# Batch 2's attention as float32 groups in a fused attention and MLP kernel

## The chip, the cores and the metric

The kernel runs on one core of a Trainium2 chip. The time is device microseconds of one execution, as a median over executions, lower is better. The engines are TensorE (PE in the profile: matmuls; PEld: its weight loads), VectorE (DVE), ScalarE (ACT), GpSimd (POOL) and SyncE (SP), which here only issues DMAs.

## The reference

Four batches, eight heads, 576 positions, head dimension 64; then two blocks on rows of 512 features. Everything is float32 in and out.

```
rel = pos[:, None] - pos[None, :]
mask_local = (rel >= 0) & (rel < 32)                     # heads 0 to 3
mask_strided = (rel >= 0) & (pos[None, :] % 32 == pos[:, None] % 32)   # heads 4 to 7
attn = softmax(where(mask, q @ k.T / 8, -1e9));  x = concat over heads of attn @ v

h = relu(x @ w_in);  u, v = halves of h;  v_n = layer norm of v
x2 = (u * (w_spatial @ v_n + b_spatial)) @ w_out

theta = x2 @ w_theta
y = x2 + w_tok_r @ (x2 * cos(theta)) + w_tok_i @ (x2 * sin(theta))
out = y + relu(y @ w_ch)
```

A position attends to at most 63 keys of its neighbourhood (local heads) or to at most 18 keys of its own class modulo 32 (strided heads, whose positions are sorted by class beforehand), so both kinds are computed in small diagonal blocks.

## The kernel before, in words

**The main work.** The matmuls of the two blocks run on float16 pairs: each float32 operand is split into a high and a low part, and three products (high·high, low·high, high·low, `PASS`) are added in PSUM. A batch's stages are, by the names of their tiles: `v` (`main_v`: 60 matmuls of 512 columns), `u`, `sp`, `x`, `th` (`main_mid`: 96, 112, 96 and 96 matmuls of 288 columns) and `y`, `c` (`main_end`: 216 and 96 of 288). The order of the stages at the end of the file is v of batch 0, then for each batch b: u, sp, x, th of b; `drain(b + 1)`; v of b + 1; y, c of b. So batch 2's attention must be done before v of batch 2, which follows th of batch 1. The stages' PSUM tiles come from one pool of three (`ps_m`). `z_chunk` takes a theta tile out of PSUM (ACT: turns; DVE: `ta<-th`, fraction), computes sine and cosine on ACT and splits z into `vn`; DMA transposes bring it to `zf`.

**Two kinds of attention.** `attention0` and `attention1(b)` work in float32, without splitting: nine groups (`groups`) of four local blocks or four to six strided blocks (one group has two local blocks). A group goes through a three-step pipeline in `attention1`: `gr_scores` (PE: two matmuls of 64 queries for each block, and the mask added by matmuls with a bfloat16 identity, into the one bank `sc`), `gr_shift` (DVE: maximum, and subtraction into `sm`), `gr_exp` (one ACT instruction), `gr_turn` (PE: transposes into the one bank `av`; ACT: copy to `pT`), `gr_pv` (PE: product with v into `av`, whose columns of ones give the sums; DVE: reciprocal and scaling), `gr_out` (PE: transposes into `sc`; ACT and DVE: high and low part into `xT`). `attention(b)` works on float16 pairs in eleven units of four blocks: `prep_qk` splits q and k (ACT: high part; DVE: low part, `qT<-qs`, `kt<-ks`), `prep_v` splits v (`vT<-vs`); `att_scores` (PE, then for each block a DVE instruction and an exponential on ACT with its sum), `att_norm` (DVE: division and low part; ACT: high part `ph`; a DMA transpose into `pT`), `att_pv` (PE, then ACT and DVE into `xT`). Batches 0 and 1 are of the first kind, batches 2 and 3 of the second: `N32` (line 33) is the number of batches in float32, and `_layout` lays the inputs out by it.

**When a step is given out.** Attention is a generator; `others` (called after each piece of main work) gives out its next step when the main work's own count of columns, divided by 2400 (`now`), has passed `ATT_AT[b][0] + n * ATT_AT[b][1]` for the n-th step (line 55). On that scale v of batch 1 lies at 59.5 to 71.0, y and c of batch 0 at 71.0 to 108.5, u to th of batch 1 at 108.5 to 156.5. A float32 attention has 13 steps, a float16 one 16. What a step gives out gets its place on each engine from the framework's scheduler, which lets `hv`, `ha`, `hg` (the main work's instructions on DVE, ACT and POOL) go 200 places ahead; so an instruction can stand earlier than the step that gave it out. All loads but three at the start go through SP's queue, in order.

The float32 attention keeps q and k in the buffers `kts` (two head pairs at a time) and v in the two buffers of tag `vT`; the float16 attention uses the same two `kts` for its split k and the same tag for its split v.

Of the kernel before, what the change touches and what calls it, by code (L numbers as in the profile page):

```python
# [29 lines left out]
TURN = 6.283185  # L30
TURNS = 1.0 / (PS * 2 * math.pi)
AHEAD = 200
N32 = 2
LAG16 = 3
V_ORDER = (0, 1, 2)
E_WAY = 'aaaadaaadaa'
# [15 lines left out]
E_YHI = 'vaavvaav'  # L52
E_ZLO = 'vvvvvvvv'
WARM = 6
ATT_AT = (None, (2.7, 3.9), (74.5, 4.4), (169.9, 4.6))
CONV_SP = (20.0, 9.9, 1.9)
CONV_OUT = (37.0, 12.0, 5.0)
CONV_TH = (49.0, 12.0, 5.0)
# [7 lines left out]
def kernel(  # L66
# [53 lines left out]
    B, DM, S = out.shape  # L120
# [28 lines left out]
    def copy(eng, key, dst, src):  # L149
        e = eng[key]  # L150
        if key == "a":
            e.activation(dst, src, AF.Copy)
        else:
            e.tensor_copy(dst, src)
# [50 lines left out]
    def pa(tag):  # L205
        return ps_a.tile([P, 512], F32, tag=tag, name=tag)

    def pa4(tag):
        return pa(tag).rearrange("p (n k) -> p n k", n=4)
# [128 lines left out]
    def prep_qk(b, hp, j, tiles):  # L338
# [7 lines left out]
        qs = att_p.tile([P, S], F32, tag="qs", name="qs")  # L346
        nc.sync.dma_start(qs, qd[b - N32, hp, :, j, :])
        ks = att_p.tile([P, S + STRIDE], F32, tag="ks", name="ks")
        nc.sync.dma_start(ks[:, 0:nk], (kl_d[b - N32, hp] if local else ks_d[b - N32, hp - 2])[:, j, :])
        copy(N, E_QHI, qT[:, j], qs)  # L350
# [78 lines left out]
    def load_qk(b, hp, q, k, c0, c1, by=None):  # L429
        by = by or nc.sync  # L430
        local = hp < 2
        src = kzl[b, hp] if local else kzs[b, hp - 2]
        k0, k1 = (c0 + STRIDE if c0 else 0, c1 + STRIDE) if local else (c0, c1)
        by.dma_start(q[:, c0:c1], qp[b, hp][:, c0:c1])
        for j in range(2):
            h = slice(64 * j, 64 * j + 64)
            by.dma_start(k[h, k0:k1], src[h, j, k0:k1])

    def load_vl(b, hp, v):
        src = vl_d[b, hp].rearrange("p n j d -> p n (j d)")  # L440
        c = slice(1, VW - 1)
        nc.gpsimd.memset(v[:, 0:9, 0:VW:VW - 1], 1.0)
        nc.sync.dma_start(v[0:96, 0:9:3, c], src[0:96, 0:6:2])
        nc.sync.dma_start(v[0:64, 1:9:3, c], src[64:128, 0:6:2])
        nc.sync.dma_start(v[64:96, 1:9:3, c], src[32:64, 1:6:2])
        nc.sync.dma_start(v[0:96, 2:9:3, c], src[32:128, 1:6:2])

    def load_vs(b, v, hps=(2, 3)):

        src = vs_d[b].rearrange("h p n j d -> p h n (j d)")  # L450
        c = slice(1, VW - 1)
        hs = slice(hps[0] - 2, hps[-1] - 1)
        for n in range(len(hps)):
            nc.gpsimd.memset(v[:, n, 0:6, 0:VW:VW - 1], 1.0)
        for i in range(11):
            k, end = CB * i, min(CB * i + CB, S)
            o = 0
            while k < end:
                n = max(range(5), key=lambda n: (SOFF[n] <= k) * (min(SOFF[n] + P, end) * 8 - n))
                m = min(end, SOFF[n] + P) - k  # L460
                p0 = k - SOFF[n]
                if i < 10:
                    r = 64 * (i % 2) + o
                    nc.sync.dma_start(v[r:r + m, :, i // 2, c], src[p0:p0 + m, hs, n])
                else:
                    for u, hp in enumerate(hps):
                        r = 64 * (hp - 2) + o
                        nc.sync.dma_start(v[r:r + m, u, i // 2, c], src[p0:p0 + m, hp - 2, n])
                k += m
                o += m  # L470
# [111 lines left out]
    def gr_out(b, g, xn, xt):  # L582
        local, blocks = groups[g]
        xh = xT[b % 2]
        for i in range(len(blocks) // 2):
            nc.tensor.transpose(xt[:, P * i:P * i + P], xn[:, i, :], ident)
        runs = []
        for i, (hp, blk) in enumerate(blocks):
            if runs and runs[-1][0] == hp and (local or blk < 10):
                runs[-1][3] += 1  # L590
            else:
                runs.append([hp, blk, i, 1])
        for hp, blk, i, n in runs:
            src = xt[:, QB * i:QB * (i + n)]
            if local:
                dst = [xh[:, e, hp, QB * blk:QB * (blk + n)] for e in range(2)]
            else:
                nr = min(3, STRIDE - 3 * blk)
                dst = [xh[:, e, hp, :].rearrange("p (j r) -> p j r", r=STRIDE)[:, :, 3 * blk:3 * blk + n * nr]
                       .rearrange("p j (n r) -> p j n r", r=nr) for e in range(2)]  # L600
                src = src.rearrange("p (n c) -> p n c", c=QB)[:, :, 0:nr * NCLS].rearrange(
                    "p n (r j) -> p j n r", j=NCLS)
            nc.scalar.activation(dst[0], src, AF.Copy)
            nc.vector.tensor_tensor(dst[1], src, dst[0], ALU.subtract)
# [56 lines left out]
    def attention1(b):  # L661
        q, k, v = {}, {}, {}

        def load_a(hp):
            q[hp], k[hp] = kts[hp % 2][:, 0], kts[hp % 2][:, 1]
            load_qk(b, hp, q[hp], k[hp], 0, S)

        def load_b(hp):
            v[hp] = att_p.tile([P, 9, VW], F32, tag="vT", name="v32", bufs=2)
            if hp < 2:  # L670
                load_vl(b, hp, v[hp])
            else:
                load_vs(b, v[hp][:, 0:6].unsqueeze(1), (hp,))

        load_a(0)
        load_b(0)
        yield
        load_a(1)
        load_b(1)
        loads = {4: (load_a, 2), 6: (load_b, 2), 7: (load_b, 3)}  # L680
        un, xs = {}, {}
        for s in range(NG + 3):
            if s < NG:
                sm = att_p.tile([P, 384], F32, tag="sm", name="sm", bufs=2)
                pT = att_p.tile([P, 4, P], F32, tag="pT", name="pT32", bufs=2)
                st = att_p.tile([P, 2, 6], F32, tag="st", name="st", bufs=4)
                un[s] = (sm, pT, st)
            if s >= 3:
                gr_out(b, s - 3, xs.pop(s - 3), pa("sc"))
            if 2 <= s < NG + 2:  # L690
                sm, pT, st = un.pop(s - 2)
                pv = pa("av")[:, 0:3 * VW].rearrange("p (i n) -> p i n", i=3)
                gr_pv(s - 2, v, pT, pv, st, pT)
                xs[s - 2] = pT
            if s < NG:
                sm, pT, st = un[s]
                sc = pa("sc")
                gr_scores(s, q, k, sc)
                gr_shift(s, sc, sm, st)
                gr_exp(s, sm)  # L700
            if s in loads:
                f, hp = loads[s]
                f(hp)
                if s == 4:
                    load_a(3)
            if 1 <= s <= NG:
                sm, pT, st = un[s - 1]
                gr_turn(s - 1, sm, pa4("av"), pT)
            yield
# [37 lines left out]
    def attention(b):  # L747
        qk, vts, pTs = {}, {}, {}
        lv = load_v(b, 0)
        prep_qk(b, 0, 0, qk)  # L750
        yield
        prep_qk(b, 0, 1, qk)
        vts[0] = prep_v(lv)
        yield
        cur = None
        qk_at = {0: (1, 0), 1: (1, 1), 3: (2, 0), 4: (2, 1), 6: (3, 0), 7: (3, 1)}
        v_at = {2: 1, 5: 2, 8: 3}
        for s in range(NU + LAG16):
            if s + 1 in v_at:
                lv = load_v(b, v_at[s + 1])  # L760
            if s >= LAG16:
                att_pv(b, s - LAG16, pTs.pop(s - LAG16), vts)
            if 1 <= s <= NU:
                pTs[s - 1] = att_norm(b, cur)
            if s < NU:
                cur = att_scores(s, qk)
            if s in qk_at:
                prep_qk(b, *qk_at[s], qk)
            if s in v_at:
                vts[v_at[s]] = prep_v(lv)  # L770
            yield
# [273 lines left out]
    timed(list(sq_parts(wth, w_th)) + [switch], *CONV_TH)  # L1045
    timed([lambda i=i: tok_part(i, (raw2, raw1)[i // 2 % 2]) for i in range(0, NZ, 2)], *CONV_TOK)
    timed(sq_parts(wch, w_ch), *CONV_CH)
    atts = [None, attention1(1)] + [attention(b) for b in range(N32, B)]
    att = {"b": 1, "n": 0}

    def now():
        return clock[0] / 2400.0
# [9 lines left out]
    def others():  # L1062
        while conv and conv[0][0] <= now():
            conv.pop(0)[1]()
        while att["b"] < B and ATT_AT[att["b"]][0] + att["n"] * ATT_AT[att["b"]][1] <= now():
            step()
# [61 lines left out]
def _layout(inputs):  # L1128
# [5 lines left out]
    def pairs(a):  # L1134
        t = a[N32:].transpose(0, 1, 3, 2).reshape(B - N32, a.shape[1] // 2, 2, D, -1)
        t = np.stack([t, t], axis=2)
        t = t.transpose(0, 1, 2, 4, 3, 5)
        return t.reshape(B - N32, a.shape[1] // 2, 2 * D, 2, -1)

    def stacked(a):  # L1140
        return a[:N32].transpose(0, 1, 3, 2).reshape(N32, a.shape[1] // 2, 2 * D, -1)

# [52 lines left out]
```

## Time and profile before

| | |
|---|---|
| median of 3 runs | 511.12 us (508.06 to 514.11) |
| the profiled execution | 509.92 us |
| its span, first to last instruction | 508.1 us |
| mean granted clock of TensorE | 0.992 of full speed |
| busy | PE 476.3 us, DVE 318.0, ACT 295.0, POOL 95.9 |

Starts are counted from the first instruction of the span; the profiled execution's time is 1.8 us longer than the span. A busy stretch of PE is the union of its matmuls' modelled times. The time that a piece of PE's work takes from the others is read from starts: from the start of its first matmul to the start of what follows. All instructions carry line 103 (a helper records them), so they are told apart by their tiles' names: `th<-x2h,wth` is a theta matmul, `sc<-kt` a float32 score, `sc<-kt,qT` a float16 score. A float32 matmul appears as two instructions.

### The profile page before, as it was taken

The page shows a single profiled execution, that of the slowest core. Times are in us where ns is not written, and L with a number is a line of the kernel's source. Part 1 is how long each engine was busy: PE and PEld are TensorE (multiplying, and loading weights), DVE is VectorE, ACT ScalarE, POOL GpSimd, SP SyncE. Part 2 cuts the span into 40 slices and gives each one's busy share as a digit, 9 for nine tenths or more (in the row PEclk, how much of TensorE's full clock was granted, in tenths as well). Part 3 has the DMA queues.
Part 4 walks back from the last instruction along what each step waited for, and adds up shares of the span by engine and source line. Part 5 has one row for each costly group of instructions (what it writes and reads, how often), then busy time and mean ns, then how long its engine had stood idle before and what let it go on. Part 6 is the DMA issues. An engine that isn't in the chain of part 4 may idle for free. (4 is left out here: it accounts for less than half of the span.)

```text
span 508.1 us, 10713 instructions
## 1 busy us (share of the span) xinstructions
PE 476.3 (94%) x4300; PEld 355.8 (70%) x4300; DVE 318.0 (63%) x714; ACT 295.0 (58%) x576; POOL 95.9 (19%) x87
## 2 busy tenths in 40 slices
PE   7889989997899789998999989999999999999996
PEld 5655757775468567776758877777657778777774
DVE  3766987557779888885399588862587121228312
ACT  2657788588995558775672767654852022158102
POOL 2042057226124410021003210021005200210220
PEclk9999999999899999998999999999999999999999
DMA  6869738456593256653170156230260020004402
GB/s 179 268 208 246 263 139 261 131 159 214 158 212 74 44 152 167 156 137 115 27 175 13 27 131 197 44 63 1 46 141 1 1 93 1 1 1 82 106 1 94
DMA packets 80296, 57.56 MB, mean 113 GB/s; under 512 B 60404, under 2 KB 66932, under 8 KB 80246
## 3 DMA queue, kind: packets, MB, share of 16 engines
q1 hardware_dynamic: 79942, 56.27, 41.4%
q8 instruction: 34, 0.56, 0.5%
q10 hardware_dynamic: 304, 0.61, 0.4%
q14 instruction: 16, 0.13, 0.1%
HBM read 37.72 MB, written 4.72 MB: 84 GB/s over the span
## 5 line engine op out<-in xcount | busy, mean ns | idle before, releaser
L103 PE MATMUL y<-wtok,zf 128*128 128x288 f16 x864 | 107.7, 286 | 1.9 <-DMA zf<-vn 1.8
L103 PEld LDWEIGHTS <-zf 128*128 128x128 f16 x864 | 83.8, 98 | 24.8 <-DMA zf<-vn 2.8
L103 PE MATMUL th<-x2h,wth 128*128 128x288 f16 x384 | 49.6, 292 | 4.7 <-DVE ta L103 4.7
L103 PE MATMUL sp<-wsp,vn 128*128 128x288 f16 x384 | 51.5, 286 | 1.6 <-ACT vn L103 1.3
L103 PE MATMUL c<-x2h,wch 128*128 128x288 f16 x384 | 48.8, 286 | 3.3 <-ACT o L103 3.3
L103 PE MATMUL x<-zf,wout 128*128 128x288 f16 x384 | 51.6, 292 | 0.0
L103 POOL TENSOR_TENSOR x2h<-x2f,x2h 128x576 f16<-128x576 f32 x20 | 26.6, 1331 | 127.8 <-issue 56.5
L103 PE MATMUL u<-xT,win 128*128 128x288 f16 x384 | 49.7, 286 | 0.0
L103 PE MATMUL v<-win,xT 128*128 128x512 f16 (+1 forms) x240 | 48.4, 380 | 0.8 <-DVE xT L103 0.6
L103 PEld LDWEIGHTS <-wth 128*128 128x128 f16 x384 | 38.1, 100 | 15.1 <-DVE ta L103 4.9
L103 PEld LDWEIGHTS <-vn 128*128 128x128 f16 x416 | 39.9, 98 | 12.1 <-ACT vn L103 1.4
L103 PEld LDWEIGHTS <-wch 128*128 128x128 f16 x384 | 37.3, 98 | 12.9 <-issue 3.8
L103 PEld LDWEIGHTS <-wout 128*128 128x128 f16 x384 | 37.3, 100 | 10.6
L103 PEld LDWEIGHTS <-win 128*128 128x128 f16 x384 | 37.3, 98 | 9.1
L103 ACT ACTIVATE sm<-sm,st 96x128 f32<-96x128 f32 (+1 forms) x88 | 34.2, 391 | 10.9 <-DVE st L103 10.8
L103 PEld LDWEIGHTS <-xT 128*128 128x128 f16 (+1 forms) x240 | 21.0, 100 | 25.2 <-issue 2.2
L103 ACT ACTIVATE x2h<-x2f 128x576 f16<-128x576 f32 (+1 forms) x28 | 20.9, 747 | 28.1 <-DVE x2f L103 27.7
L103 POOL TENSOR_TENSOR zf<-u,zf 128x576 f16<-128x576 f32 x8 | 10.7, 1339 | 107.8 <-ACT zf L103 105.1
L103 DVE SCALAR_TENSOR_TENSOR x2f<-y,x2f 128x576 f32<-128x576 f32 x16 | 12.0, 752 | 26.2 <-PE y L103 26.1
L103 ACT ACTIVATE o<-c 128x576 f32<-128x576 f32 (+1 forms) x17 | 10.3, 612 | 30.3 <-PE c L103 30.0
L103 DVE TENSOR_TENSOR ta<-ta,x2f 128x1152 f32<-128x1152 f32 x16 | 21.5, 1353 | 10.1 <-ACT ta L103 10.1
L103 DVE TENSOR_TENSOR u<-u,sp 128x576 f32<-128x576 f32 x16 | 12.0, 750 | 23.4 <-PE sp L103 23.3
(140 smaller groups left out, 780.5 us busy)
## 6 DMA issues: line engine op xcount, KB each, us to landing
qs<-in_qd_dram SPq DMA_DIRECT2D x16, 288.0 KB
out_dram<-o SPq DMA_DIRECT2D x15, 288.0 KB
ks<-in_kl_dram SPq DMA_DIRECT2D x8, 304.0 KB
ks<-in_ks_dram SPq DMA_DIRECT2D x8, 288.0 KB
x2f<-in_w_in_dram SPq DMA_DIRECT2D x2, 1024.0 KB
zf<-in_w_in_dram SPq DMA_DIRECT2D x2, 1024.0 KB
xT<-in_w_ch_dram SPq DMA_DIRECT2D x2, 1024.0 KB
vs<-in_vl_dram SPq DMA_DIRECT2D x4, 384.0 KB
```

The costliest lines, as they stand in the source:

```text
L103: ins = f(*args, **kwargs)
```

## The change

Batch 2's attention is made by `attention1(2)` in place of `attention(2)`. Its 13 steps are given out from 79.0 on, one each 5.4 (to 143.8), in place of 16 steps from 74.5 on, one each 4.4 (to 140.5). `_layout` puts batch 2's q, k into the float32 layout. Batches 0, 1 and 3 keep their kind and their times.

```
-N32 = 2
+N32 = 3
...
-ATT_AT = (None, (2.7, 3.9), (74.5, 4.4), (169.9, 4.6))
+ATT_AT = (None, (2.7, 3.9), (79.0, 5.4), (169.9, 4.6))
...
-    atts = [None, attention1(1)] + [attention(b) for b in range(N32, B)]
+    atts = [None] + [attention1(b) for b in range(1, N32)] + [attention(b) for b in range(N32, B)]
```

DVE at the theta stage of batch 0, before: `xT_95<-sc` ends batch 1's attention, `kt`, `qT` and `vT` split batch 2's first q, k and v, the `ISA` rows are its first blocks' masks and maxima.

```order
L103 TENSOR_TENSOR xT_95<-sc,xT_95 128x18x12
L103 TENSOR_TENSOR kt_80<-ks,kt_80 128x608
L103 TENSOR_TENSOR qT<-qs,qT 64x576
L103 SCALAR_TENSOR_TENSOR vT<-vs,vT 128x768
L103 ISA sm,st<-sc,mask 96x128
L103 ISA st 96x1
```

The same place now; `wx` is a weight conversion, the three `ta` take theta tiles out of PSUM, the last two rows are the first group's maxima and subtraction (`gr_shift`).

```order
L103 TENSOR_TENSOR xT_95<-sc,xT_95 128x18x12
L103 SCALAR_TENSOR_TENSOR wx<-xT_94,wx 128x576
L103 SCALAR_TENSOR_TENSOR ta_1549<-th_1493,ta_1549 128x576
L103 SCALAR_TENSOR_TENSOR ta_1566<-th_1494,ta_1566 128x576
L103 SCALAR_TENSOR_TENSOR ta_1602<-th_1577,ta_1602 128x576
L103 TENSOR_REDUCE st<-sc 128x4
L103 TENSOR_TENSOR sm<-sc,st 128x384
```

The three splits and two blocks' masks stood between `xT` and the conversion with the theta tiles behind it; now nothing stands between, and attention's DVE work comes after the theta tiles.

PE at the end of the y stage of batch 0, now: the product with v of group 0 (`av<-v`), the scores of group 2 and their masks, then the `c` matmuls.

```order
L103 MATMUL y_2005<-wtok,zf 128x288
L103 MATMUL av<-v_1854,pT_1928 64x65 x8
L103 MATMUL sc<-kt_81 64x96 x8
L103 LDWEIGHTS identb
L103 MATMUL sc<-mask_100,identb 128x96
L103 LDWEIGHTS identb
L103 MATMUL sc<-mask_100,identb 128x288
L103 LDWEIGHTS wch
L103 MATMUL c_2098<-x2h,wch 128x288
```

Before, the same place held 12 float16 products with v (`av<-pT,vT`) and the 8 float16 scores of a unit (`sc<-kt_81,qT`).

DVE in the sp stage of batch 1, now: `u` gates, `xT`, `st`, `pT`, `sm` of batch 2's groups, and the splits of batch 3's k and v (`kt<-ks`, `vT<-vs`).

```order
L103 TENSOR_TENSOR u_2346<-u_2346,sp_2590 128x576
L103 TENSOR_TENSOR kt_81<-ks,kt_81 128x608
L103 TENSOR_TENSOR u_2414<-u_2414,sp_2622 128x576
L103 TENSOR_TENSOR xT_94<-sc,xT_94 128x18x18
L103 TENSOR_SCALAR st<-av 128x6
L103 RECIPROCAL st<-st 128x6
L103 TENSOR_TENSOR pT_2417<-av,st 128x384
L103 TENSOR_REDUCE st<-sc 128x4
L103 SCALAR_TENSOR_TENSOR vT<-vs,vT 128x768
L103 TENSOR_TENSOR sm<-sc,st 128x256
```

Batch 3's splits keep their place by time, and now stand among the instructions of batch 2's groups in place of those of its float16 units.

## Rows read from the trace of the kernel before

**Rows 1.** The page: busy us (share of the span), instructions.

```profile
PE 476.3 (94%) x4300; PEld 355.8 (70%) x4300; DVE 318.0 (63%) x714; ACT 295.0 (58%) x576; POOL 95.9 (19%) x87
```

**Rows 2.** Timeline of PE, stage starts: start us, us, line, operation, tiles, count.

```profile
144.91 17.82 PE L103 MATMUL y<-wtok,zf 128*128 128x288 f16 x144
...
252.03 11.94 PE L103 MATMUL v<-win,xT 128*128 128x512 f16 x60
263.91 13.40 PE L103 MATMUL y<-wtok,zf 128*128 128x288 f16 x108
...
351.59 11.92 PE L103 MATMUL th<-x2h,wth 128*128 128x288 f16 x96
363.35 11.94 PE L103 MATMUL v<-win,xT 128*128 128x512 f16 x60
```

**Rows 3.** PE's waits, 118.3 to 252: us in total, times, longest us.

```profile
PE th L103 <- DVE ta L103: 4.7, 1, 4.7
PE sc L103 <- DVE st L103: 3.8, 2, 3.4
PE av L103 <- DVE xT L103: 2.5, 1, 2.5
PE c L103 <- ACT o L103: 1.1, 1, 1.1
```

**Rows 4.** Timeline of PE around the two stalls with a slow clock after them.

```profile
122.97 0.87 PE L103 MATMUL sc<-kt,qT 128*96 128x128 f16 x8
128.56 4.64 PE L103 MATMUL th<-x2h,wth 128*128 128x288 f16 x24 [4.72 <-DVE ta L103]
...
230.25 0.52 PE L103 MATMUL av<-pT,vT 128*64 128x126 f16 x12 [2.53 <-DVE xT L103]
230.71 6.23 PE L103 MATMUL x<-zf,wout 128*128 128x288 f16 x36
```

**Rows 5.** Stretches, PE alone: us, PE busy (instructions), granted clock, DMA share, GB/s.

```profile
127.70:131.10 3.40, 2.54 (x11) 0.59 0.80 261
...
230.00:234.00 4.00, 3.75 (x26) 0.59 0.95 260
```

**Rows 6.** Timelines of DVE and ACT in the theta stage of batch 0.

```profile
121.76 1.58 DVE L103 TENSOR_TENSOR kt<-ks,kt 128x608 f16<-128x608 f32 x1
...
126.42 1.40 DVE L103 SCALAR_TENSOR_TENSOR wx<-xT,wx 128x576 int32<-128x576 int32 x1
127.75 2.07 DVE L103 SCALAR_TENSOR_TENSOR ta<-th,ta 128x576 f32<-128x576 f32 x3
...
120.25 0.69 ACT L103 ACTIVATE kt<-ks 128x608 f16<-128x608 f32 x1
...
122.16 1.15 ACT L103 ACTIVATE wtok<-wx 128x1152 f16<-128x1152 f32 x1
...
123.81 0.71 ACT L103 ACTIVATE wx<-xT 128x576 int32<-128x576 uint8 x1
```

**Rows 7.** Timeline of PE in batch 1's attention: first full group, last product.

```profile
48.78 0.88 PE L103 MATMUL sc<-kt 64*64 64x96 f32 x16
49.59 0.34 PE L103 MATMUL sc<-mask,identb 128*128 128x384 bf16 x1
49.76 0.60 PE L103 MATMUL av<-ident,sm 128*96 128x128 f32 x4
...
118.19 4.94 PE L103 MATMUL th<-x2h,wth 128*128 128x288 f16 x39
```

**Rows 8.** The stretch of batch 1's attention, PE alone, columns as in rows 5.

```profile
48.78:118.19 69.41, 65.31 (x702) 1.00 0.62 202
```

**Rows 9.** PE's waits, 48.7 to 118.3, columns as in rows 3.

```profile
PE sp L103 <- ACT vn L103: 1.3, 1, 1.3
PE sc L103 <- DVE sm L103: 1.1, 2, 0.7
PE sc L103 <- DVE xT L103: 0.6, 2, 0.4
PE av L103 <- DVE pT L103: 0.5, 1, 0.5
PE sp L103 <- POOL vn L103: 0.3, 1, 0.3
PE av L103 <- DVE rs L103: 0.2, 1, 0.2
```

**Rows 10.** Groups by form: busy us, mean ns of one, idle before.

```profile
L103 PEld LDWEIGHTS sc<-kt 64*64 64x64 f32 x168 | 6.7, 133 | 4.2 <-issue 2.3 <-DVE sm L103 1.0 <-DVE xT L103 0.6
...
L103 DVE TENSOR_TENSOR kt<-ks,kt 128x608 f16<-128x608 f32 x8 | 10.7, 1341 | 0.1
```

## The prediction

> **What bounds the kernel now.** I read the page first: PE is busy for 476.3 of 508.1 us and no other engine for more than 318.0 [rows 1], so the end is set by how long PE's own sequence takes and by the holes in it. The change therefore has two sides: float32 groups cost PE more matmul time than float16 units, and they may take away holes.
>
> The timeline of PE shows what the stages cost. Batch 3's 96 theta matmuls take from 351.59 to 363.35, 11.76 us, or 0.1225 us each [rows 2]. That is less than the 11.92 us which the row calls busy: the last matmul's modelled end lies 0.16 us behind the next one's start, so a real hole is 0.16 us longer than the profile's idle figure. From y of one batch to the end of theta of the next are 216 + 96 + 96 + 112 + 96 + 96 = 712 such matmuls, 87.2 us. The stretch that carries batch 2's attention lasts 252.03 - 144.91 = 107.1 us, the one that carries batch 3's 363.35 - 263.91 = 99.4 us [rows 2]. So the same float16 attention adds 19.9 us to the one and 12.2 us to the other: the difference is holes. PE's waits name them: 3.8, 2.5 and 1.1 us inside batch 2's stretch, and 4.7 us just before it, in the theta stage of batch 0, where PE waits for the DVE instruction that frees a theta tile [rows 3].
>
> Two of the holes cost more than their length. After the 4.72 us hole 24 matmuls take 4.64 us where 24 x 0.1225 + 0.16 = 3.10 is usual, after the 2.53 us hole 36 take 6.23 where 4.57 is usual [rows 4]: 1.5 and 1.7 us. In both places the granted clock is 0.59 on average over the stretch [rows 5], that is, part of it at 1.2 in place of 2.4 GHz.
>
> So batch 2's attention as it is costs: 19.9 us in its stretch; in the theta stage 128.56 - 122.97 = 5.6 us from its first scores to the next theta matmul [rows 4]; and 1.5 us of slow clock. **Together 27.0 us.** About 10.7 of these are PE's own work, batch 3's 12.2 less its one 1.5 us hole.
>
> **The change, part by part.**
>
> *PE's work added.* Batch 1's attention is the same program as batch 2's will be. From the first full group's scores at 48.78 to the theta matmul after its last product at 118.19 are 69.41 us [rows 7]. In between stand 96 u, 112 sp, 96 x and 33 theta matmuls, 337 x 0.1225 = 41.3 us. PE is busy for 65.31 of it [rows 8], so 4.1 us are idle, in eight pieces [rows 9], which with 8 x 0.16 make 5.4. What is left is 22.7 us. Group 0 was scored before; its scores cost as much as the next group's, 49.76 - 48.78 = 1.0 [rows 7]. Float32 attention thus takes **23.7 us of PE without its waits**, 13.0 more than the float16 one. This includes what each break in a run of float16 matmuls costs and the hidden weight loads.
>
> One rule speaks against such a step. A float32 weight load takes 133 ns on average [rows 10], yet 16 scores with their loads take 49.59 - 48.78 = 0.81 us, 51 ns each [rows 7]: the loads lie beside other work. The Trainium skill ("TensorE: Matmul & The Clock Gate", section "Weight-path perf modes") says that the fast weight load is not used for float32. If the loads were exposed, 160 scores would cost 160 x (133 - 51) = 13 us more; the row already contains whatever they cost, so I keep 23.7.
>
> *The theta stage.* DVE's chain before: batch 2's splits begin at 121.76, and with two blocks' masks they hold DVE until the conversion at 126.42; the theta tile follows at 127.75 [rows 6]. The order of the change has none of this in front. The conversion then waits for ACT alone. There k, q and v splits go (from 120.25 to 122.16, 1.9 us), so the ACT conversion that ended at 124.5 ends at 122.6, or at 123.3 if the conversion ahead of it waits for DVE. Add DVE's 1.3 us (127.75 - 126.42) and 0.7 for the first of three theta instructions: 124.6 to 125.4. PE reaches this point at 122.97 + 1.0 (group 0's scores) = 123.95. A hole of 0.7 to 1.5 us stays; I take **1.5 with the 0.16**, from the upper end since POOL's conversions also pass there. Bounds: 0, and the whole 4.9 if something else holds the tile.
>
> *Batch 2's own stalls.* The 3.8, 2.5 and 1.1 us [rows 3] belong to the float16 chain: exponentials block by block, the splits, the `o` of stage c behind exponentials on ACT. They go. In their place come the hand-offs of the one `sc` and the one `av` bank, for each group six passes between PE and DVE or ACT. Batch 1 shows their price: waits of 1.1, 0.6, 0.5 and 0.2 us in six pieces [rows 9], 3.4 us with the 0.16. There DVE and ACT also convert weights. Batch 2 has none of that after its first group, but batch 3's splits. I take half, **1.7 us**; bounds 0.3 and 3.4, and the rival below for more.
>
> *DMA.* Eleven transposes of probabilities and 16 larger loads of q and k become some 46 smaller loads on SP's queue. Batch 1 made the same loads between weight loads, and PE waited for none of them in its stretch [rows 9]. I count nothing: between the last scores from a `kts` buffer and the first from its next contents the new order has 60 main matmuls, 7.4 us. If that cover is too short, each of the two refills costs the rest.
>
> *Batch 1's stretch.* Batch 2's first splits of q, k and v stood on DVE and ACT there. Batch 3's first two q splits take the place of batch 2's, but k and v splits go. I count -0.4 us, between 0 and -1.
>
> *The sum.* 23.7 + 1.5 + 1.7 = 26.9 us against 27.0, and -0.4: **-0.5 us**. From the profiled execution's 509.92 this gives 509.4. The median of the runs, 511.12, lies 1.2 above that execution, so I forecast **510.5 us** for a median. The holes bought 13.0 us and the float32 matmuls spend them.
>
> **Rivals.**
>
> *Faster: the holes vanish altogether.* The new order cuts the float16 runs into fewer pieces than in batch 1, theta does not wait, banks are always free: 23.7 - 0.8 + 0 + 0.3 = 23.2, -1.0 in batch 1, and -0.5 in batch 3, whose q splits come earlier. That is -5.3 us, 505.5. For it: DVE and ACT lose more than 20 us of work here. Against: batch 1 shows six waits in nine groups.
>
> *Slower: batch 3's splits sit in the bank chain.* In the sp and x stages DVE has four `kt` and two `vT` splits of batch 3 among the groups' steps, each of which holds the only `sc` or `av` bank. A `kt` split takes 1.34 us on average [rows 10], 1.58 in the theta stage [rows 6]. If six of them lie on the chain, 8 us, and one such hole brings a slow clock of 1.7: +9.7 - 1.7 - 0.5 = +7.5, 518.6. It decides from 2.2 us of hand-off waits on for slower at all, from 7.3 on for over 1%. Against: the sp order leaves PE 18 to 28 main matmuls (2.2 to 3.4 us) after most scores.
>
> *The theta stall stays.* If ACT's or POOL's conversions held the tile, not DVE's splits, 4.9 in place of 1.5 and the slow clock again: +4.9, less 0.5, 515.5. For it: POOL's conversions end late there. Against: DVE's rows put the splits right ahead of the conversion and the theta tile [rows 6].
>
> *A short hole is enough for a slow clock.* The trace has a slow spell after 2.53 us of idling but none after the 3.4 us one [rows 3, 4]. If the 1.5 us hole brings one too, +1.5: 512. The Trainium skill (the page named, section "Part 1: The HAM clock gate") says that idling brings the clock down to half; this trace agrees in two places (0.59, rows 5) and shows that length alone does not decide.
>
> **How the numbers follow.** Forecast within some 3 us of 510.5: 0.62. Holes vanish: 0.13. Splits in the chain: 0.11. Theta stall or clock: 0.14, nearly all of it within 1%. Over 1% (5.1 us, about what a measurement of this kernel can tell from no change): faster 0.12, slower 0.12, same 0.76. The range takes in the bounds (-4.5 from hand-offs, theta and batch 1; +5 from theta and hand-offs) around 510.5, widened by 1 to 2 us, as single runs before lay 3 us on either side of their median: 504 to 517.
>
> **What would show it.** Right: the wait of theta for `ta` near 128 falls to 0.7 to 1.5 us without a slow spell; y to theta of batch 1 lasts 110.5 to 113 us in place of 107.1, with waits of `sc` and `av` below 3.4 us in all; batch 3's stretch stays at 99.4. Wrong: waits of PE on `kt` loads, a slow clock in the sp or x stage, or float32 pieces longer than in batch 1.

## The result, and the profile after

The changed kernel takes 506.47 us (median of 20 runs, 504.17 to 509.03), the kernel before 511.99 on the same chip (20 runs, 508.06 to 517.15). The ratio is 0.9902, 95% interval 0.988 to 0.9924: 1.0% faster, just at the bound that I had drawn between no change and faster. The time lies inside my range, 4 us below my forecast. The profiled execution takes 506.96 us, with a span of 505.1.

The page of the changed kernel, busy time, answers to [rows 1]:

```profile
PE 485.1 (96%) x4460; PEld 364.4 (72%) x4460; DVE 284.8 (56%) x607; ACT 267.8 (53%) x475; POOL 92.9 (18%) x91
```

PE works 8.8 us longer, in a span that is 3.0 us shorter. PE's waits from theta of batch 0 to v of batch 2, against [rows 3]:

```profile
PE th L103 <- DVE ta L103: 2.0, 1, 2.0
PE sc L103 <- DVE xT L103: 0.4, 1, 0.4
```

[rows 3] begins at 118.3; with a wait of 0.4 us of `sc` for `xT` just ahead of it, the kernel before has 12.5 us. Of these 2.4 are left. The timeline of PE: group 0's scores, the theta tile that waits, and the two ends of batch 2's stretch [rows 2, 4].

```profile
122.56 0.88 PE L103 MATMUL sc<-kt 64*64 64x96 f32 x16
123.37 0.34 PE L103 MATMUL sc<-mask,identb 128*128 128x96 bf16 x2
125.73 3.56 PE L103 MATMUL th<-x2h,wth 128*128 128x288 f16 x15 [2.02 <-DVE ta L103]
...
142.10 1.15 PE L103 MATMUL y<-wtok,zf 128*128 128x288 f16 x8
...
250.10 11.94 PE L103 MATMUL v<-win,xT 128*128 128x512 f16 x60
```

The stretch lasts 108.00 us where it lasted 107.1. The theta tile's place and that stretch by windows, PE alone, columns as in rows 5:

```profile
125.50:128.90 3.40, 3.17 (x14) 0.50 0.74 259
142.10:250.10 108.00, 108.00 (x1077) 1.00 0.26 73
```

In batch 2's stretch PE is never idle. The theta hole of 2.02 us has a stretch at 0.50 (1.2 GHz) behind it. Its chain on ACT and DVE:

```profile
121.25 0.73 ACT L103 ACTIVATE xT<-xT 128x576 f32<-128x576 f32 x1 [1.65 <-DMA xT<-in_w_ti_dram]
...
122.94 0.72 ACT L103 ACTIVATE wx<-xT 128x576 int32<-128x576 uint8 x1
...
123.69 1.32 DVE L103 SCALAR_TENSOR_TENSOR wx<-xT,wx 128x576 int32<-128x576 int32 x1 [2.60 <-ACT wx L103]
124.94 1.41 DVE L103 SCALAR_TENSOR_TENSOR ta<-th,ta 128x576 f32<-128x576 f32 x2
```

Read upwards, the theta tile waits for DVE's conversion, that for ACT's, and that for the load of w_ti. Batch 2's splits, which had this place in [rows 6], are gone, and DVE idles for 2.60 us.

### The profile page after: what moved, and what is told of

The parts are those of the page before. It is cut to its first block, busy times and chain, and to the rows that moved or that the text cites. A ratio compares the mean times of both kernels' runs of the same rounds, so it can differ in the third digit from the quotient of the medians.

```text
span 505.1 us, 10834 instructions
## 1 busy us (share of the span) xinstructions
PE 485.1 (96%) x4460; PEld 364.4 (72%) x4460; DVE 284.8 (56%) x607; ACT 267.8 (53%) x475; POOL 92.9 (18%) x91
## 3 DMA queue, kind: packets, MB, share of 16 engines
HBM read 35.36 MB, written 4.72 MB: 79 GB/s over the span
## 5 line engine op out<-in xcount | busy, mean ns | idle before, releaser
L103 PE MATMUL y<-wtok,zf 128*128 128x288 f16 x864 | 107.2, 286 | 1.0 <-DMA zf<-vn 1.0
L103 PE MATMUL x<-zf,wout 128*128 128x288 f16 x384 | 49.9, 286 | 0.0
L103 POOL TENSOR_TENSOR x2h<-x2f,x2h 128x576 f16<-128x576 f32 x20 | 25.5, 1279 | 119.1 <-ACT x2h L103 47.2
L103 PEld LDWEIGHTS <-wth 128*128 128x128 f16 x384 | 38.1, 100 | 12.5 <-issue 2.2
L103 ACT ACTIVATE o<-c 128x576 f32<-128x576 f32 (+1 forms) x17 | 10.4, 616 | 32.1 <-PE c L103 31.8
L103 POOL TENSOR_TENSOR zf<-u,zf 128x576 f16<-128x576 f32 x8 | 10.7, 1340 | 86.0 <-ACT zf L103 86.0
L103 DVE TENSOR_TENSOR vn<-ta,vn 128x1152 f16<-128x1152 f32 x16 | 21.5, 1355 | 5.6 <-ACT vn L103 5.6
```

Of the source, the lines that this page charges most:

```text
L103: ins = f(*args, **kwargs)
```

## The experiments

The first theory: the kind of attention makes the gain. The first rival: the new table of due times makes it.

**E1 and E2: the two halves of the change apart.** E1 is the kernel before with the new table, E2 the changed kernel with the old table.

```
E1, against the kernel before:    E2, against the changed kernel:
-... (74.5, 4.4), ...             -... (79.0, 5.4), ...
+... (79.0, 5.4), ...             +... (74.5, 4.4), ...
```

> Batch 2's attention stays on float16 pairs, but its 16 steps are given out from 79.0 on, one each 5.4, as the change does. Theory (the gain comes from the kind: float16 splits no longer stand ahead of the theta tiles, and the float16 chain's holes in batch 2's stretch go): the splits still stand ahead of the theta conversion on VectorE, so the theta hole of 4.7 us stays, and the time is that of the kernel before, ratio 0.995 to 1.005. Rival (the pacing alone makes the gain, since the steps meet better gaps): ratio 0.988 to 0.993.

> Batch 2's attention in float32 groups, given out by the old table (74.5 on, one each 4.4). Theory (kind): most of the gain is there, ratio 0.988 to 0.994; batch 2's stretch lasts about 108 us as after the change, the theta wait is near 2 us. Rival (pacing): groups bunch, hand-offs of the two banks make PE wait over 2 us in the stretch, ratio 0.997 or more.

E1: 509.34 us, ratio 0.9959 (0.9934 to 0.9985). E2: 513.02 us, ratio 1.0031 (0.9999 to 1.0063). E1's theory holds and its rival falls: the table alone brings 0.4%, not the gain. E2's theory falls: the kind alone brings nothing. E2's rival comes true in its numbers, a ratio above 0.997 and a wait of PE of over 2 us for a bank, though one group's place makes it, as its timelines show, and not a bunching of groups. Neither half makes the gain. E1's longest waits of PE, theta of batch 0 to y of batch 1:

```profile
PE th L103 <- DVE ta L103: 5.8, 2, 4.7
PE av L103 <- DVE xT L103: 2.0, 1, 2.0
PE v L103 <- DVE ta L103: 1.7, 1, 1.7
```

With the later table the float16 units miss the 3.4 us hole of the y stage [rows 3]; the theta hole of 4.7 stays, and the end of the sixteen steps now runs into theta and v, where 1.1, 1.7 and 2.0 us are lost. E2's theta wait is 1.6 us, near the 2 expected, but PE loses 4.2 us in the y stage. Its timelines there (DVE, ACT, PE):

```profile
159.42 2.36 DVE L103 TENSOR_SCALAR vr<-vr,mv,rs 128x512 f32<-128x512 f32 x5
...
160.90 2.52 ACT L103 ACTIVATE vn<-vr 64x512 f16<-64x512 f32 x3 [4.89 <-DVE vr L103]
...
164.32 0.59 ACT L103 ACTIVATE pT<-av 96x512 f32<-96x512 f32 x1
...
164.97 0.74 PE L103 MATMUL av<-v,pT 96*64 96x65 f32 x16 [4.21 <-ACT pT L103]
```

The copy `pT<-av` frees the only `av` bank; it stands on ACT behind `vn<-vr`, which waits 4.89 us for the layer norm of v on DVE. A float32 group that begins in front of the layer norm holds its bank until the norm is done. In the changed kernel the first y-stage scores come at 162.0, and their instructions on DVE follow the norm.

**E3: batch 3 in float32 too.**

```
-N32 = 3
+N32 = 4
...
-ATT_AT = (None, (2.7, 3.9), (79.0, 5.4), (169.9, 4.6))
+ATT_AT = (None, (2.7, 3.9), (79.0, 5.4), (176.0, 5.4))
```

> Batch 3's attention in float32 groups too, its steps given out from 176.0 on, one each 5.4. Theory (what was won with batch 2 are its float16 holes, 7 us inside its stretch and 5 us at theta, while float32 costs 11 us more of matmuls): batch 3's float16 attention has only 1.5 us of holes, so its stretch grows from 99.7 to 108 to 109 us, and the time is 8 to 9 us above the changed kernel's, ratio to before 1.004 to 1.009. Rival (float32 groups are cheaper as such, because they take work off VectorE and ScalarE): ratio to before 0.985 or less.

516.66 us, ratio 1.0107 (1.0075 to 1.0139): 10.2 us above the changed kernel, where the expectation had 8 to 9 and a ratio of at most 1.009. Batch 3's stretch on PE's timeline:

```profile
260.40 1.77 PE L103 MATMUL y<-wtok,zf 128*128 128x288 f16 x13
...
369.83 1.46 PE L103 MATMUL v<-win,xT 128*128 128x512 f16 x6
```

109.4 us in place of 99.7. Where float16 has few holes to lose (1.5 us), float32 costs nearly its full price. The rival falls.

**E4 and E11: each kernel once more, unchanged.** E4 is the kernel before, E11 the changed one.

> The kernel before once more, for another profile of it. Theory (the profiled execution of before fell on the fast side: the distance of the medians is 5.5 us, that of the two profiles 3.0, because the three long holes and the slow-clock stretches behind them differ from execution to execution): the holes at theta (4.7), batch 2's x stage (2.5) and batch 3's sp stage (3.4) stand again, but their lengths or the slow stretches behind them add up to 1.5 us more or less than in the first profile. Rival (executions differ in the tail or the loads, not in these holes): holes and slow stretches the same within 0.3 us, the difference elsewhere.

> The changed kernel once more, for a second profile and a second ratio. Theory (the holes are those of the order and stand in each execution; only the slow-clock stretches behind them come and go): theta wait 1.9 to 2.2 us, no other wait over 0.7 us from th of batch 0 to v of batch 2, a stretch at 1.2 GHz behind theta or none; ratio to before 0.988 to 0.993. Rival (the first comparison was luck of the executions): ratio 0.995 or more.

E4 took 511.21 us; E11 504.87 (4 runs), ratio 0.9886 (0.9836 to 0.9936). E4's theta tile and its slow windows:

```profile
131.46 5.34 PE L103 MATMUL th<-x2h,wth 128*128 128x288 f16 x24 [4.72 <-DVE ta L103]
```

```profile
129.20:136.00 6.80, 4.54 (x20) 0.50 0.68 223
173.60:180.40 6.80, 5.80 (x29) 0.50 0.30 71
233.00:240.00 7.00, 6.21 (x67) 1.00 0.64 180
```

```profile
174.60 1.01 PE L103 MATMUL sc<-kt,qT 128*96 128x128 f16 x8 [3.42 <-DVE st L103]
```

The holes at theta (4.72) and in the y stage (3.42; the expectation puts it into batch 3's sp stage by mistake) are the same to 0.01 us in both executions. The clock behind them is not. In the first profile it falls behind theta and behind the x hole of 2.53 us [rows 5], not behind the y hole; in E4 behind theta and y, not behind an x hole of 1.62. E11's theta tile, and the windows of theta and of batch 2's stretch:

```profile
125.32 3.10 PE L103 MATMUL th<-x2h,wth 128*128 128x288 f16 x24 [1.64 <-DVE ta L103]
```

```profile
125.20:128.90 3.70, 3.58 (x27) 1.00 0.79 279
140.10:248.30 108.20, 108.14 (x1076) 1.00 0.27 76
```

The order is the same, the hole 1.64 in place of 2.02 us, less than the 1.9 to 2.2 expected, and no slow stretch follows. The 24 theta matmuls then take 2.94 us to the next start (128.26), where the first profile took 4.49. At 0.50 a slow stretch should cost half of what PE was busy in it, an estimate that fits the 1.55 us between 4.49 and 2.94: 1.6 us in the first profile of the changed kernel and 0 in E11, 3.3 and 5.2 in the two of the kernel before.

E4's theory falls all the same. From theta to y of batch 1, waits and slow clock add up to 15.8 us in the first profile and 15.5 in E4 (the table below), where it asked for a difference of 1.5. The difference lies elsewhere, as the rival has it, though the single holes and slow stretches are not the same: theta of batch 0 begins at 116.11 in place of 113.37. Ahead of it E4's clock fell twice:

```profile
20.00:26.80 6.80, 6.70 (x74) 0.50 0.63 195
67.80:71.20 3.40, 3.40 (x16) 0.50 0.00 0
```

E4's v matmuls begin at 34.64. E5, the only other profile with a slow clock between 12 and 60 us (0.51 from 22.8 to 29.7), begins them at 35.07, the other twelve between 31.66 and 32.67.

**E5 and E7: float16 with its first splits behind theta.** The splits of q, k and v of batch 2's first heads must follow the third theta tile on their engine; E7 adds a later table.

```
+            if b == 0 and m == 2:
+                last.update(a=ti, v=tf)
...
+        if b == 2 and hp == 0:
+            tc.add_manual_dep(ins.ins, last[eng].ins.name, ...)
...
E7: -... (74.5, 4.4), ...
    +... (82.0, 4.4), ...
```

> The kernel before (float16 pairs, old table), but batch 2's first splits of q, k and v must stand behind the third theta tile's instructions on ScalarE and VectorE. Theory (the gain has two parts, the theta hole, which batch 2's first splits make on VectorE, and the hole in the y stage, where attention steps meet the layer norm of v; kind and table each remove one): the theta wait falls from 4.7 us to 2 to 3, the 3.4 us wait for st in the y stage stays or grows, and about 1 to 3 us are won, ratio 0.993 to 0.999. Rival (the theta hole alone makes the gain): ratio 0.988 to 0.992. Rival (the theta hole is ScalarE's or GpSimd's conversions, not the splits): wait of 4 us or more, ratio 1.000.

> As the run before the last: float16 pairs with the first splits behind theta, and a later table too (82.0 on, one step each 4.4), so that the first scores come behind the layer norm and the last step still before theta. Theory (it is holes that were won, and float16 pairs cost 11 us less of TensorE than float32 groups): theta wait 2 to 3 us, no wait over 1.5 us in the y stage, the stretch from y to v lasts 98 to 102 us in place of the changed kernel's 108.0, ratio to before 0.974 to 0.985, faster than the change. Rival (float16 pairs bring holes wherever they stand, by their many instructions on VectorE and ScalarE): stretch 104 us or more, ratio 0.990 or more.

E5: 511.99 us, ratio 1.0028 (0.9997 to 1.0059). Its waits of PE:

```profile
PE th L103 <- DVE ta L103: 2.9, 1, 2.9
PE av L103 <- DMA pT<-ph: 2.5, 1, 2.5
PE sc L103 <- DVE qT L103: 2.3, 1, 2.3
PE sc L103 <- DVE kt L103: 1.5, 1, 1.5
```

The splits do hold the theta tile: its wait falls from 4.7 to 2.9 us. From the first theta matmul to this tile's are 15.2 us before, 12.6 in E5, and 12.9 and 12.5 in the two profiles of the changed kernel, so the splits account for all that the change won there. But they then stand in the y stage with the layer norm, and scores wait for `qT` and `kt`: the waits sum to 12.0 us, little less than the 12.5 before, and the expected 1 to 3 us are not won. E7: 512.87 us, ratio 1.0033 (1.0012 to 1.0054), with one wait of 7.9 us in the y stage; the theory falls, and the rival comes true in its numbers (ratio 0.990 or more; from y to v 112.6 us, where it has 104 or more). DVE and PE there:

```profile
167.84 2.60 DVE L103 TENSOR_TENSOR kt<-ks,kt 128x608 f16<-128x608 f32 x1
170.37 1.21 DVE L103 TENSOR_TENSOR vn<-vr,vn 128x1024 f16<-128x1024 f32 x1
...
175.80 1.01 PE L103 MATMUL sc<-kt,qT 128*96 128x128 f16 x8 [7.89 <-DVE st L103]
```

**E6 and E9: the last theta hole of the changed kernel.** The last part of w_ti gets a free piece of `zf` as its buffer; E9 adds a later table.

```
+    raw3 = zf[:, 4 * S + 5120:8 * S + 5120].bitcast(I64)
-... tok_part(i, (raw2, raw1)[i // 2 % 2]) ...
+... tok_part(i, (raw2, raw1, raw2, raw1, raw3)[i // 2]) ...
E9: -... (79.0, 5.4), ...
    +... (85.0, 5.1), ...
```

> The changed kernel with the last token weights (w_ti) loaded into a free part of zf, so that the load no longer waits for the buffer of the conversion before it. Theory (the theta wait of 2.0 us that is left, and the stretch at 1.2 GHz behind it, come from ScalarE's conversion, which waits 1.65 us for this load): the theta wait falls below 0.6 us, the slow stretch goes, 1.5 to 3.5 us less than the changed kernel, ratio to before 0.982 to 0.988. Rival (the theta tile is held by the whole chain of conversions, the load is only the first of several late steps): wait stays at 1.5 us or more, ratio that of the change, 0.988 to 0.992.

> The changed kernel with the early load of w_ti and a later table for batch 2 (85.0 on, one step each 5.1): no scores of batch 2 stand before the 162nd y matmul, so none needs VectorE while it works on the layer norm of v. Theory (two places make holes, the conversions at theta and the layer norm in the y stage; the early load clears the first, the later table the second): theta wait below 1.2 us, no wait over 1 us in the y stage, y to v of batch 2 lasts 107 to 109 us, theta to v of batch 1 13.6 us; about 3 us less than the changed kernel, ratio to before 0.981 to 0.987. Rival (a hole that is filled in one place opens in the next, whatever the table): another wait of 2 us or more between y and v, ratio 0.990 or more.

E6: 510.58 us, ratio 0.9988 (0.9966 to 1.001), so neither expectation's time came. The theta wait falls to 0.9 us, not below the 0.6 expected, and no slow stretch follows; the tile's matmuls come 10.7 us behind the first theta matmul in place of 12.9 and 12.5, so the load was the cause of most of the hole. But the order moved with it: group 0's scores left theta for the y stage, in front of the layer norm. DVE and PE there:

```profile
162.11 1.22 DVE L103 TENSOR_TENSOR vn<-vr,vn 128x1024 f16<-128x1024 f32 x1
163.24 0.55 DVE L103 TENSOR_REDUCE st<-sc 128x4 f32<-128x384 f32 x1
...
164.53 0.88 PE L103 MATMUL sc<-kt 64*64 64x96 f32 x16 [4.48 <-DVE sm L103]
```

It is E2's hole again, now at the `sc` bank. E9's later table removes it. PE's waits, theta of batch 0 to y of batch 1:

```profile
PE th L103 <- DVE ta L103: 0.9, 1, 0.9
PE sc L103 <- DVE xT L103: 0.3, 1, 0.3
```

Yet E9 takes 506.75 us, ratio 0.9916 (0.9889 to 0.9944): no faster than the change. The expected 3 us were 1.6 of a slow stretch, which E11 lacks without this edit, and 1.65 of waiting, of which E11's 1.64 leaves 0.8 to win. From theta of batch 0 to y of batch 1 E9 takes 147.1 us, E11 147.4. Behind that E9's profile loses 1.9 us, and two waits there are longer by as much: `c` waits 3.4 us for ACT's `o` (2.4 in E11), `y` 1.9 us for a DMA into `zf` (1.0). So a hole did open elsewhere, behind the stretch that the rival named.

**E8: work in the hole, nothing else.** 34 matmuls whose result nothing reads, in front of the theta tile that waits, in the kernel before.

```
+            if b == 0 and m == 3:
+                fill = pa("av")
+                for _ in range(34):
+                    nc.tensor.matmul(fill[:, 0:HS], wth[:, 0, 0, 0:P], x2h[:, 0, 0, 0:HS], start=True, stop=True)
```

> The kernel before with 34 extra matmuls of 288 columns, whose result nothing reads, in front of the theta tile that waits 4.7 us: they work for 4.2 us in the place where TensorE idled. Theory (the stretch at 1.2 GHz behind theta comes from the idling, and costs 1.6 to 2.3 us each time): theta's matmuls behind it run at 2.4 GHz, and 1.5 to 2.5 us are won although no wait was removed, ratio 0.994 to 0.998. Rival (the slow stretch has another cause, or costs nothing in the end): ratio 1.000 or more, the slow stretch still there.

PE's timeline and windows:

```profile
124.68 4.33 PE L103 MATMUL av<-x2h,wth 128*128 128x288 f16 x34
130.17 3.10 PE L103 MATMUL th<-x2h,wth 128*128 128x288 f16 x24 [1.16 <-DVE ta L103]
```

```profile
130.00:133.50 3.50, 3.33 (x26) 1.00 0.84 275
166.50:173.30 6.80, 5.13 (x27) 0.50 0.00 0
```

The theta matmuls run at 2.4 GHz, in the one place where four of four profiles with the 4.72 us hole (before, E1, E4, E12) have 0.50. So the idling makes the slow stretch here. The time, 511.20 us, ratio 1.0003 (0.9982 to 1.0024), shows no gain: the fillers pushed the first scores into the y stage, where the hole grew to 4.9 us and brought its own slow stretch. The gain in time is thus neither shown nor excluded.

**E10: float16 behind the layer norm.** E7 with E6's buffer, and a table that puts batch 2's first scores into stage c.

```
-... (74.5, 4.4), ...
+... (90.0, 4.1), ...
```

> Batch 2 on float16 pairs with its first splits behind theta, the early load of w_ti, and a table (90.0 on, one step each 4.1) that puts its first scores into the c stage, behind the layer norm. Theory (float16 pairs cost 11 us less of TensorE; the holes are those of places, and this table meets neither): no wait over 1.5 us from y to v, which lasts 98 to 102 us, ratio to before 0.970 to 0.980. Rival (float16 pairs keep VectorE too busy between y and theta, so that scores wait for st wherever they stand): waits of sc and av of 4 us or more in the stretch, 103 us or more, ratio 0.983 or more.

510.05 us, ratio 0.9975 (0.9952 to 0.9997). PE's waits:

```profile
PE c L103 <- ACT x2h L103: 5.8, 1, 5.8
PE v L103 <- DVE ta L103: 2.5, 1, 2.5
```

The scores are out of the way, the splits are not: the norm, `kt` and `qT` splits and the y tiles share DVE until 177, ACT's `x2h<-x2f` comes late, and now stage c waits. At the end attention runs into theta and v, as in E1. The theory falls. The rival has the stretch (107.2 us, where it has 103 or more) and the ratio right, but not the place: the long wait is that of `c`, not of scores.

**E12: the kernel before with two weight conversions less.**

```
-    wch = const.tile([P, 2, NC, DM], F16, name="wch")
+    wch = wth
...
-    timed(sq_parts(wch, w_ch), *CONV_CH)
```

> The kernel before without the conversion and load of the last weight, w_ch: the c matmuls read w_theta's high and low parts in its place, so two conversions (two ScalarE passes of 1.1 us, a third of 1.0 and a VectorE pass of 1.2 each, with GpSimd's low parts) are left out between theta of batch 0 and the y stage; TensorE's order is that of before, word for word. Theory (batch 2's place differs from batch 3's, whose float16 attention has one hole of 1.5 us, by the weight conversions that share VectorE and ScalarE with the layer norm and the splits in the y stage): the wait of sc for st at the y stage falls from 3.4 us to below 1.5, and y to v of batch 2 from 107.1 to 104 us or less. Rival (splits and layer norm alone overfill VectorE there): that wait stays at 2.5 us or more, y to v at 105.5 us or more.

This kernel leaves `w_ch` out: its c matmuls multiply by `w_theta`, so it computes something else than the reference. PE's waits, theta of batch 0 to v of batch 2:

```profile
PE th L103 <- DVE ta L103: 4.7, 1, 4.7
PE av L103 <- DVE xT L103: 3.6, 3, 2.5
PE c L103 <- ACT o L103: 1.5, 1, 1.5
PE sc L103 <- DVE st L103: 0.4, 1, 0.4
```

508.90 us, ratio 0.9937 (0.9912 to 0.9963). With the same order on TensorE the y-stage wait falls from 3.4 to at most 0.4 us, which the theory asked; y to v falls only to 105.0 us, where 104 or less was asked, since the x hole of 2.5 stays, with a slow clock behind it. So batch 2's place differs from batch 3's, where the same float16 attention has 1.5 us of holes, in part by the weight conversions beside it.

**All profiles side by side**, from theta of batch 0 to y of batch 1 (the third y stage), in us. Slow clock is half of PE's busy time in stretches at 0.50; the last column is the total less waits and slow clock. E8's rest holds its 34 fillers, some 4.2 us.

| | kind of batch 2 | total | waits of PE | slow clock | rest |
|---|---|---|---|---|---|
| before | float16 | 150.5 | 12.5 | 3.3 | 134.7 |
| E4 before again | float16 | 149.7 | 10.3 | 5.2 | 134.2 |
| E1 new table | float16 | 150.1 | 10.4 | 4.6 | 135.1 |
| E5 splits behind theta | float16 | 151.6 | 12.0 | 5.1 | 134.5 |
| E7 E5, table 82.0 | float16 | 151.9 | 14.6 | 3.2 | 134.1 |
| E10 E7, table 90.0 | float16 | 150.3 | 12.0 | 3.1 | 135.2 |
| E12 no w_ch | float16 | 149.7 | 10.8 | 4.4 | 134.5 |
| E8 fillers | float16 | 150.0 | 9.1 | 2.6 | 138.3 |
| after | float32 | 149.1 | 2.4 | 1.6 | 145.1 |
| E11 after again | float32 | 147.4 | 2.0 | 0 | 145.4 |
| E2 old table | float32 | 153.9 | 6.2 | 1.6 | 146.1 |
| E3 batch 3 too | float32 | 147.7 | 2.4 | 0 | 145.3 |
| E6 early w_ti | float32 | 152.7 | 5.8 | 1.7 | 145.2 |
| E9 E6, table 85.0 | float32 | 147.1 | 1.2 | 0 | 145.9 |

The account closes: whatever the order, the rest is 134 to 135 us with float16 (E8 without its fillers too) and 145 to 146 with float32. The change costs 10.8 us of PE (mean of the two profiles of each kernel), takes away 9.2 us of waits and 3.4 of slow clock: -1.9 us with the rounding. No float16 order of the table came below 10.3 us of waits, but for E8, which fills part of one; float32 has 2.4 or less wherever its first y-stage scores stand behind 162 of the 216 y matmuls, and 5.8 and 6.2 where they stand behind 126 and 108 (E6, E2), in front of the norm.

## Why the prediction was right, and where its steps were not

**Right: the balance.** I forecast that the float32 matmuls spend what the holes bought, and a change within 1%. The holes go, PE's work comes, and what is left is 1.0%, at the very edge of that case. But the case with 0.62, within some 3 us of 510.5, did not come: 506.47 is 4.0 away, and the change is -5.5 us where I had -0.5. The width of the range took it in. Nearest lies the rival of vanishing holes (0.13) with 505.5, though theta still waits. Of the four signs of being right two came (waits of `sc` and `av` below 3.4 us, batch 3's stretch 99.7 for 99.4) and two did not: theta's wait, and y to theta in 110.5 to 113 us, which took 108.0.

**Two sums of the prediction are off.** Its bounds from hand-offs, theta and batch 1 below the forecast are 1.4, 1.5 and 0.6, together 3.5 us and not 4.5; the range would begin at 505 to 506, and the time would still lie in it. The rival of vanishing holes, -5.3 us from 511.12, is at 505.8, not 505.5.

**The float32 price was too high.** "23.7 us of PE without its waits, 13.0 more than the float16 one": batch 2's stretch is 108.0 - 87.2 = 20.8 us of attention with no idle time, and with 1.0 for group 0's scores 21.8. The table gives 10.8 more than float16. Batch 1's stretch, from which I took the price, holds some 2 us that batch 2's does not have. Both hold the same attention matmuls (362 instructions in either trace), but PE changes between main work and attention 59 times in batch 1's stretch and 42 times in batch 2's. That these breaks cost the 2 us was not tried.

**The hand-off stalls were mis-sized.** I took 1.7 us, half of batch 1's; they are 0. The rival of batch 3's splits in the bank chain fell with them: the only hand-off wait, 0.4 us, belongs to batch 1's last group.

**The theta hole had the right size and another cause.** I took 1.5 with the 0.16; the wait is 2.02 and 1.64 in two executions. The splits held the tile (E5), as I read from [rows 6]; most of what is left is not POOL's conversions but the load of w_ti (E6). The rival of a slow clock behind a short hole came true in one of two profiles.

**The executions of the kernel before were taken for one.** Its slow clock was 3.2 us in my sum and cost 3.3 and 5.2 us in two profiles. The medians differ by 5.5 us, the mean spans of the two profiles of each kernel by 4.5: 1.9 by the table, 0.6 behind it (from y of batch 1 to the last matmul), and 1.9 ahead of theta, most of it in E4, where the clock fell twice. Batch 1's stretch, where I counted -0.4, went from 69.41 to 68.75.

How often the slow clock comes is on record, as the mean granted clock of every run: 0.994 in the 20 runs of the changed kernel (0.987 to 1.000), and 0.980 to 0.984 in the four sets of 10 to 31 runs of the kernel before, 81 in all, that stand beside the experiments (single runs 0.972 to 0.997). At 0.50 in the slow stretches that makes, by an estimate (twice the missing share of the span), 6 us of slow clock in the changed kernel and 17 to 21 in the kernel before. The profile that I took my rows from has 0.992, which only 10 of those 81 runs reach. So the profiles show where 2.5 of the 5.5 us come from. What the slow clock is worth in the rest stays open: by a straight line through each set, 10 us more of it go with 0.5 to 1.4 us more of time in the kernel before, and with 3.5 us in the changed one.

**The step that was missing: the table.** I priced the kind and counted nothing for the new due times. E2 shows that the kind with the old table is no gain at all (1.0031), because its first groups meet the layer norm. E1 shows that the table alone is worth 0.4%.

## What to carry to other kernels

An attention step that holds a single PSUM bank must not begin in front of a long chain on the engine that frees it: place it behind the layer norm, and look at every later edit for whether the scheduler moved it back (E6). To judge a cheaper engine sequence, split each profile into work, waits and slow clock; here the work of either kind came out the same, within some 1 us, in every order tried, and only the other two moved. And take two profiles of each kernel, and look at the granted clock of all its runs, before crediting an edit with a clock stretch.

## What the runs showed of the hardware that I had not expected

**The same hole does not always bring the slow clock.** The 1.3 us wait of the first sp matmuls for ACT, near 65, is in most profiles; E4, E6, E8 and E12 have 0.50 behind it, the two profiles of the changed kernel, the first of before, E1, E2 and E9 have 1.00. Behind the 3.4 us hole of the y stage before ran at 1.00 (171.00 to 175.00) and E4 at 0.50. The length of one hole does not decide it alone.

**VectorE and GpSimd slow each other down.** DVE and POOL in the y stage of the kernel before:

```profile
166.25 1.22 DVE L103 TENSOR_TENSOR vn<-vr,vn 128x1024 f16<-128x1024 f32 x1
167.38 2.71 DVE L103 TENSOR_TENSOR kt<-ks,kt 128x608 f16<-128x608 f32 x1
...
166.26 3.19 POOL L103 TENSOR_TENSOR vn<-vr,vn 128x1024 f16<-128x1024 f32 x1 [1.26 <-ACT vn L103]
169.41 1.82 POOL L103 TENSOR_TENSOR x2h<-x2f,x2h 128x576 f16<-128x576 f32 x1
```

This `kt` split, right ahead of the scores that wait 3.4 us, takes 2.71 us, with POOL at work beside it all the time. Of the sixteen `kt` splits in that profile eleven take 0.74 to 0.79 us; ten of these have no POOL work beside them, and the eleventh began ahead of POOL's. The five long ones, 1.20 to 2.71 us, all began while a POOL instruction ran, and ended 0.6 to 0.7 us behind its end. POOL's `vn` takes 3.19 where it takes 2.24 in E12. The Trainium skill ("SBUF — State Buffer", section "Who interferes with whom") says that a VectorE instruction with two SBUF inputs contends with a GpSimd instruction that reads SBUF, and calls the contention for their shared ports an exclusive lock; the five long `kt` splits agree with that. It is one more reason why float16's splits, all of two SBUF inputs, were dear in the y stage.
